# Staggering the batch rows of a two-layer decode kernel so that part of K and V is read once

## The chip, the cores and the metric

The kernel runs on one core of one Trainium2 chip. The metric is the device time of one execution in microseconds (us). Below, "median" is the median of the fast runs of a kernel. TensorE multiplies matrices, VectorE, ScalarE and GpSimd work on elements, and SyncE issues the transfers. In the profile they are called PE (and PEld for the weight loads of TensorE), DVE, ACT, POOL and SP.

## The reference, cut to what matters

```python
# x (8,1,448); K and V caches (8,8,4096,256) bf16; 16 query heads, 8 KV heads
x = x + attn(layernorm(x), K, V, wq, wo)   # layer 0
x = x + B(layernorm(x), w1, w2, w3, w4)
x = x + attn(layernorm(x), K, V, wq, wo)   # layer 1: the same caches and weights
x = x + B(layernorm(x), w1, w2, w3, w4)
```

It is one decode step. Each batch row has its own K and V and never meets another row. K and V of all rows are 256 MiB together, and both layers read the same ones, so a kernel that keeps nothing reads 512 MiB. With one token the gating branch of `B` (w1 and w2) contributes nothing, and both kernels leave it out.

The second layer of a row needs the first layer's result of that row. Between the two there is a chain of small dependent steps: softmax sums, output projection, normalisation, MLP, normalisation again, query projection, and spreading of the query into the layout that the scores need. I call it *the chain* below.

## The kernel before

It takes all rows through layer 0 and then all rows through layer 1. K and V arrive in pieces of 1 MiB; there are three buffers of 2 MiB for K and five of 1 MiB for V. A scheduler orders the instructions. Cuts are marked with `# ...`.

```python
    kp = ctx.enter_context(tc.tile_pool(name="kp", bufs=3))
    vp = ctx.enter_context(tc.tile_pool(name="vp", bufs=5))
    # ...
    def load_k(b, g):
        t = kp.tile([128, 32, Dh], BF16, tag="k")
        src = A_k_cache[b, g].rearrange("(p c) d -> p c d", c=32)
        for n in range(2):                      # 8 KB per partition and transfer
            nc.sync.dma_start(t[:, 16 * n : 16 * n + 16], src[:, 16 * n : 16 * n + 16])
        return t

    def load_v(b, g, hh):
        t = vp.tile([128, 2, 8 * Dh], BF16, tag="v")
        nc.sync.dma_start(                      # two runs of 4 KB per partition
            t[:],
            A_v_cache[b, g, 2048 * hh : 2048 * hh + 2048].rearrange(
                "(a p y) d -> p a (y d)", a=2, y=8
            ),
        )
        return t
    # ...
    units = [(ly, b, g) for ly in range(2) for b in range(Bn) for g in range(G)]
    # ...
    for n, (ly, b, g) in enumerate(units):
        if b == 0 and g == 0:
            emit_q(0, Bn)                       # queries of all rows
        load(n + 1)
        # ...
        transpose_k(kt)                         # DVE, in place, 2 x 2.31 us
        scores(sc, kt, qbd, g)
        pt = probs(sc, zall, g)
        pv(o_ps, pt, v0, 0, g)
        pv(o_ps, pt, v1, 1, g)
        if g == G - 1:
            finish_attention(b, o_ps, zall)
            if b == Bn - 1:
                emit_wo(0, Bn)                  # once per layer, 8 rows at a time
                emit_mlp(0, Bn)
```

The chain thus runs once between the layers, for eight rows at a time, and once at the end without its query part.

The softmax here doesn't subtract the row's maximum and nothing guards it: scores larger than these inputs give would overflow.

## Time and profile before

| | before |
|---|---|
| median (lowest to highest) | 1407.51 us (1407.33 to 1409.43), 4 runs |
| span of the profiled execution | 1405.5 us |
| read from HBM | 547.43 MB |
| chain that ended last | DMA 93% |

Here are lines of the page of the kernel before. The first two give the span and, per engine, busy us, share of the span and instructions (x). The two in the middle cut the span into 40 equal slices of 35 us: busy share of DMA in tenths, and GB/s. The last is the chain of work that ended last, by engine.

```profile
span 1405.5 us, 29105 instructions
PE 577.4 (41%) x13414; PEld 426.9 (30%) x13414; DVE 628.4 (45%) x439; ACT 125.6 (9%) x391; POOL 10.2 (1%) x14
...
DMA  9999999999999999999929999999999999999980
GB/s 327 399 414 414 413 415 413 415 413 414 415 414 414 415 413 414 413 415 412 414 121 370 413 413 415 413 414 415 414 414 414 414 414 413 414 414 414 414 345 1
...
HBM read 547.43 MB, written 0.01 MB: 389 GB/s over the span
...
DMA 93%; PE 4%; DVE 2%; issue 0%; POOL 0%; ACT 0%; POOLq 0%; SPq 0%; ACTq 0%; DVEq 0%
```

The stream is the limit: DMA runs at 412 to 415 GB/s everywhere but at the start, in slices 21 and 22 (121 and 370 GB/s) and in the tail, where nothing is left to load. Every compute engine is busy less than half of the time. The Trainium skill, "DMA: Bandwidth & Descriptors" (Specifications), gives about 358 GB/s of HBM for one core and 435 for the fabric; this trace has 412 to 415 with one core running, so the second figure is the nearer one here.

SyncE's waits show the same. The columns are what it waited for, us in total, number of waits, and the longest.

```profile
SPq L305 <- DMA t<-in_A_v_cache_dram: 480.8, 244, 2.9
SPq L305 <- PE o_ps L364: 230.6, 110, 38.3
```

The waits are many and short: apart from three for the weights at the start (up to 19.0 us), one for the output at the end and one of 38.3 us, none is longer than 3.0 us. The one of 38.3 us is the gap between the layers. The timeline of the gap shows what a chain consists of. Columns: start us, duration us, engine, line, operation, shapes, count, and in brackets the idle time before.

```profile
694.78 7.97 PE L239 MATMUL y_ps<-wo_sb,OT 128*8 128x448 bf16 x32 [0.39 <-DVE OT L385]
...
708.56 2.90 POOL L168 TENSOR_TENSOR rs<-ve,nhalf 128x16 f32<-128x16 f32 x1 [688.52 <-DVE ve L165]
...
715.97 4.21 PE L286 MATMUL y_ps<-w_sb,HT 128*8 128x448 bf16 x14 [2.13 <-DVE HT L283]
...
729.75 3.58 PE L205 MATMUL q_ps<-t,wq_sb 128*128 128x8 bf16 x128 [5.37 <-DVE t L192]
```

The output projection takes 7.97 us, one inverse square root on GpSimd 2.90 us, the second MLP product 4.21 us, and the query projection 3.58 us. The steps follow each other, and from the softmax sums (691.7) to the first new scores (735.5) they fill about 44 us.

### The profile page before, as it was taken

What the parts mean: (1) busy time and instruction counts of PE and PEld (TensorE: products, weight loads), DVE (VectorE), ACT (ScalarE), POOL (GpSimd) and SP (SyncE); (2) the same over time, 40 slices, a digit from 0 to 9 for tenths busy, and PEclk for the clock granted to TensorE, in tenths of its full rate; (3) what the DMA queues carried; (4) which work ended last, traced back from release to release, by engine and by line L of the source; (5) the groups of instructions that cost most, each with busy time, mean ns of one, the idle gap of its engine ahead of it and who ended that gap; (6) DMA issues with size and microseconds to landing.
All of it is one profiled execution on the core that took longest, in us unless ns stands there. A gap on an engine that the chain in (4) does not pass through costs nothing.

```text
span 1405.5 us, 29105 instructions
## 1 busy us (share of the span) xinstructions
PE 577.4 (41%) x13414; PEld 426.9 (30%) x13414; DVE 628.4 (45%) x439; ACT 125.6 (9%) x391; POOL 10.2 (1%) x14
## 2 busy tenths in 40 slices
PE   2234343343434334343554433434343343434336
PEld 2223233232323323232333332323233232323323
DVE  2254444444454444445444444444544444454441
ACT  0101000010101010010001000101010100101010
POOL 0000000000000000000010000000000000000000
PEclk9999999999999999999955555555555555555556
DMA  9999999999999999999929999999999999999980
GB/s 327 399 414 414 413 415 413 415 413 414 415 414 414 415 413 414 413 415 412 414 121 370 413 413 415 413 414 415 414 414 414 414 414 413 414 414 414 414 345 1
DMA packets 113753, 549.32 MB, mean 391 GB/s; under 512 B 8400, under 2 KB 14432, under 8 KB 80480
## 3 DMA queue, kind: packets, MB, share of 16 engines
q1 hardware_dynamic: 107120, 540.59, 94.6%
q10 hardware_dynamic: 6512, 6.88, 1.5%
q8 instruction: 105, 1.72, 0.5%
q14 instruction: 16, 0.13, 0.0%
HBM read 547.43 MB, written 0.01 MB: 389 GB/s over the span
## 4 chain that ended last, share of the span: by engine, by line
DMA 93%; PE 4%; DVE 2%; issue 0%; POOL 0%; ACT 0%; POOLq 0%; SPq 0%; ACTq 0%; DVEq 0%
DMA t<-in_A_k_cache_dram 89%; DMA wo_sb<-in_A_wo_dram 2%; DMA w_sb<-in_B_w_dram 1%; PE y_ps L239 1%; DVE t L318 1%; PE y_ps L286 1%; PE sc_94 L325 0%; PE st L144 0%; POOL rs L168 0%; PE o_ps L364 0%; PE q_ps L205 0%; PE ps L127 0%; PE h_ps L263 0%; POOLq L469 0%; ACT y_sb L250 0%
## 5 line engine op out<-in xcount | busy, mean ns | idle before, releaser
L318 DVE STREAM_TRANSPOSE t<-t 128x2048 uint32<-128x2048 uint32 x256 | 589.3, 2308 | 622.2 <-DMA t<-in_A_k_cache_dram 313.9
L325 PEld LDWEIGHTS <-qbd 128*8 128x8 bf16 x4096 | 130.4, 115 | 674.0 <-issue 594.9
L364 PE MATMUL o_ps<-pt,t 128*128 128x2 bf16 x8192 | 238.7, 165 | 45.3 <-ACT pt L353 39.1
L364 PEld LDWEIGHTS <-t 128*128 128x128 bf16 x8192 | 238.3, 104 | 57.2 <-issue 48.8
L325 PE MATMUL sc_93<-t,qbd 128*8 128x256 bf16 x2048 | 120.2, 410 | 320.9 <-DVE t L318 319.7
L325 PE MATMUL sc_94<-t,qbd 128*8 128x256 bf16 x2048 | 120.5, 410 | 296.3 <-DVE t L318 296.3
L335 ACT ACTIVATE p_sb<-sc_93 128x256 bf16<-128x256 f32 x64 | 47.1, 736 | 585.2 <-PE sc_93 L325 585.2
L335 ACT ACTIVATE p_sb<-sc_94 128x256 bf16<-128x256 f32 x64 | 47.1, 736 | 549.8 <-PE sc_94 L325 549.8
L345 PE MATMUL pt_ps<-identb,p_sb 128*128 128x32 bf16 x256 | 30.1, 198 | 123.5 <-ACT p_sb L335 123.5
L345 PEld LDWEIGHTS <-p_sb 128*128 128x128 bf16 x256 | 16.8, 110 | 186.9 <-ACT p_sb L335 186.9
L384 DVE RECIPROCAL rz<-z_ps 128x16 f32<-128x16 f32 x16 | 4.1, 258 | 63.2 <-PE z_ps L376 63.2
L353 ACT CAST pt<-pt_ps 128x64 bf16<-128x64 f32 x128 | 27.1, 212 | 49.0 <-PE pt_ps L345 49.0
L227 DVE TENSOR_SCALAR qbd<-qs,quad 128x128 bf16<-128x128 f32 x64 | 19.2, 345 | 17.0 <-PE qs L222 17.0
L168 POOL TENSOR_TENSOR rs<-ve,nhalf 128x8 f32<-128x8 f32 (+1 forms) x4 | 9.1, 2271 | 1362.6 <-DVE ve L165 1342.2
L335 ACT ACTIVATION_READ_ACCUMULATOR p_sb<-sc_94 128x1 f32 x64 | 16.7, 261 | 0.0
L335 ACT ACTIVATION_READ_ACCUMULATOR p_sb<-sc_93 128x1 f32 x64 | 16.7, 261 | 0.0
L239 PE MATMUL y_ps<-wo_sb,OT 128*8 128x448 bf16 x64 | 16.2, 424 | 0.8 <-DVE OT L385 0.8
L376 PE MATMUL z_ps<-zall,hsel 128*128 128x8 f32 x64 | 16.0, 361 | 0.0
L376 PEld LDWEIGHTS z_ps<-zall,hsel 128*128 128x128 f32 x64 | 14.9, 322 | 0.0
L205 PE MATMUL q_ps<-t,wq_sb 128*128 128x8 bf16 x256 | 7.6, 168 | 14.2 <-DVE t L192 8.7
L252 DVE TENSOR_TENSOR xT<-xT,ps 128x32 f32<-128x32 f32 x4 | 0.7, 187 | 25.5 <-PE ps L131 25.5
L205 PEld LDWEIGHTS <-wq_sb 128*128 128x128 bf16 x256 | 7.2, 104 | 14.5 <-issue 6.1
(80 smaller groups left out, 92.1 us busy)
## 6 DMA issues: line engine op xcount, KB each, us to landing
t<-in_A_k_cache_dram SPq DMA_DIRECT2D x256, 1024.0 KB, 20.2
t<-in_A_v_cache_dram SPq DMA_DIRECT2D x256, 1024.0 KB, 20.0
wo_sb<-in_A_wo_dram ACTq DMA_DIRECT2D x1, 3584.0 KB, 31.8
wq_sb<-in_A_wq_dram SPq DMA_DIRECT2D x3, 1024.0 KB, 8.9
w_sb<-in_B_w_dram ACTq DMA_DIRECT2D x1, 1568.0 KB, 20.1
w_sb<-in_B_w_dram ACTq DMA_DIRECT2D x3, 448.0 KB, 4.1
wq_sb<-in_A_wq_dram SPq DMA_DIRECT2D x2, 256.0 KB, 12.9
w_sb<-in_B_w_dram ACTq DMA_DIRECT2D x2, 112.0 KB, 4.2
```

The lines of the kernel that those rows point to most:

```text
L168: nc.gpsimd.tensor_tensor(rs[:, 0:n, :].rearrange("p n b -> p (n b)"), ve[:, 0:n, :].rearrange("p n b -> p (n b)"), nhalf[:, 0 : n * nb], ...
L205: nc.tensor.matmul(q_ps[:, j * Hq + h, :], w, xb[:, xi, :], start=(fc == 0), stop=(fc == 3),)
L227: nc.vector.tensor_scalar_mul(qbd[:, :, :, a, :], qs[:].rearrange("p e (f g h) -> p (e f) g h", f=2, h=2), quad[:, a : a + 1],)
L239: nc.tensor.matmul(y_ps[:], OT[:, j, h, b0 : b0 + nb], wo_sb[:, grp, :], start=(grp == 0), stop=(grp == NB2 - 1),)
L286: nc.tensor.matmul(y_ps[:], HT[:, c * nb : c * nb + nb], w4_sb[:, c, :], start=(c == 0), stop=(c == HC - 1),)
L318: nc.vector.transpose(w, w)
L325: nc.tensor.matmul(sc[32 * k : 32 * k + 8, :], qbd[:, ep, g].rearrange("p a h -> p (a h)"), kv[:, k, 2 * half + e2, par], start=(ep == 0), ...
L335: nc.scalar.activation(p_sb[:].rearrange("p t i x -> p x t i"), sc[:].rearrange("p (x t i) -> p x t i", x=4, t=2), ACT.Exp, scale=scale_ex ...
L345: nc.tensor.matmul(pt_ps[:, t], p_sb[:, t].rearrange("p i x -> p (i x)"), rows, start=True, stop=True,)
L353: nc.scalar.copy(pt[:], pt_ps[:])
L364: nc.tensor.matmul(o_ps[:, g, j, :], v[:, a % 2, y * Dh + 128 * j : y * Dh + 128 * j + 128], pt[:, t, k, 2 * a : 2 * a + 2], start=(first ...
L376: nc.tensor.matmul(z_ps[:, h, :], hsel[:, h : h + 1].to_broadcast([128, 128]), zall[:], start=True, stop=True,)
```

## The change: its intent and the diff

The intent is to read less. A row's second pass starts soon after its first, so that part of the row's K and V can stay in SBUF between the two. K and V of a row are 32 pieces of 1 MiB. Those of its last head pair, four of K and four of V, are kept, so that 64 MiB of the 512 MiB need not be read. Now the chain has to run once per row, that is eight times, while other rows' pieces stream. So the change cuts it into a generator with 18 steps and runs two of them after each piece. Order is now written by hand, and the memory that was K and V buffers becomes a ring of six slots of 1 MiB and eight kept slots. Also, V comes in runs of 8 KB per partition. The diff, cut to its core:

```diff
-    kp = ctx.enter_context(tc.tile_pool(name="kp", bufs=3))
-    vp = ctx.enter_context(tc.tile_pool(name="vp", bufs=5))
+    NS = 6
+    kept = [(GP - 1, kv, n) for n in range(4) for kv in range(2)]
+    ctx.enter_context(tc.manual_schedule())
+    slots = [consts.tile([128, 16 * Dh], BF16, name=f"slot{n}") for n in range(NS + len(kept))]
 ...
+    def out_rows(lhs, w, n, b0, nb):            # output projection, and w4 of the MLP
+        y_ps = ps_m.tile([nb, D], FP32, tag="m")
+        for i in range(n):
+            nc.tensor.matmul(y_ps[:], lhs(i), w[:, i, :], start=(i == 0), stop=(i == n - 1))
+            if i % 16 == 15:
+                yield
+        y_sb = chn.tile([Bn, D], FP32, tag="y_sb")
+        nc.scalar.copy(y_sb[:nb, :], y_ps[:])
+        yield
+        ps = rows_to_cols(y_sb, nb)
+        xs = xT[:, :, b0 : b0 + nb]
+        nc.vector.tensor_add(xs, xs, ps[:])
 ...
+    def chain(b, st):
+        OT = work.tile([128, 2, Hq], BF16, tag="OT")
+        yield from finish_attention(st["o"], st["z"], OT)
+        yield from out_rows(lambda i: OT[:, i % 2, i // 2 : i // 2 + 1], wo_sb, NB2, b, 1)
+        yield from mlp(b, 1)
+        qT = chn.tile([128, NB2], BF16, tag="qT2")
+        yield from project_q(b, 1, qT[:].unsqueeze(2))
+        qbd = work.tile([128, 8, GP, 4, 2], BF16, tag="qbd", bufs=3)
+        yield from spread_q(qT[:], qbd)
+        state[1, b] = {"q": qbd}
 ...
-    units = [(ly, b, g) for ly in range(2) for b in range(Bn) for g in range(G)]
+    tasks = [(0, 0, gp) for gp in range(GP)]
+    for b in range(1, Bn):
+        tasks += [(1, b - 2, gp) for gp in range(GP - 1)] if b > 1 else []
+        if b == 1:
+            tasks += [(0, 1, gp) for gp in range(GP - 1)]
+            tasks += [(1, 0, keep), (0, 1, keep)]
+        else:
+            tasks += [(1, b - 1, keep)]          # from the kept slots, not from HBM
+            tasks += [(0, b, gp) for gp in range(GP)]
 ...
+    for idx, it in enumerate(items):             # one item = one piece of K or V
+        n, kv, c = it
+        ...
+        if kv == 0:
+            ...
+            if not (ps == 1 and (gp, 0, c) in kept):
+                transpose_k(slot)
+            scores(sc_t[n % 2], slot, c, st["q"], gp)
+            ...
+        else:
+            pv(state[ps, b]["o"], pt_of[n], slot, c, gp)
+        ...
+        if not (ps == 0 and (gp, kv, c) in kept):
+            held[where[it]] = False
+        emit_loads()
+        for _ in range(2):                       # two steps of the chain per piece
+            for g in gens:
+                next(g, None)
```

The scores of a piece are now 32 products of 128 columns instead of 256, since a piece is 1 MiB and not 2 MiB. The final output projection and MLP still run for eight rows at once after the stream.

## The prediction

> **What bounds it now.** The page's chain is 93% DMA; its slices show DMA at 9 tenths and 412 to 415 GB/s except in three places: the start (327 GB/s), the gap between the layers (121, then 370 GB/s in slices 21 and 22) and the tail (nothing after about 1364 us of 1405). PE (41%), DVE (45%) and ACT (9%) have room. So time is about 512 MiB of K and V at 2.53 us per MiB (1297 us), 26 us of weights, 28 us of DMA lost between the layers, 41 us of tail, about 10 us of start.
>
> **What the change takes away.**
> 1. 64 of 512 MiB: each row's last head pair stays in SBUF: 64 x 2.53 = 162 us.
> 2. V is now read in pieces of 8 KB per partition, not 4 KB. In the trace's DMA packets, stretches of K (8 KB) ran at about 419 GB/s, stretches of V (4 KB) at about 408; all at 419 is 2.50 us per MiB: another 13 us.
> 3. The gap between layers: 28 us. The tail stays (final projection and MLP of 8 rows, 32 us, are unchanged): minus 4 us.
>
> With nothing added this would be about 1195 us.
>
> **What it adds.** The chain from attention to the next layer's q now runs eight times, once per row, cut into 18 steps, two after each 1 MiB piece, on the engines that must also free the slots. It is nearly as long for one row as for eight: read from the gap between layers (timeline): output projection 8.0 us, copy 0.5, back to columns 1.1, statistics 1.7, norm 1.7, w3 1.7, GELU 2, w4 4.2, copy and columns 1.7, second norm 3.5, q 3.6, spreading 2; some 38 us with the doubled softmax sums. The rsqrt on POOL took 1.64 us for 8 columns and 2.90 for 16, so I estimate 0.7 for a row.
>
> The Trainium skill, "TensorE: Matmul & The Clock Gate" (What happens when you issue a matmul), says that only weight loads move ahead on TensorE and matmuls stay in program order; its queue-depth paragraph calls ScalarE and VectorE strictly first in, first out. The program order of the changed kernel puts transposes (2.31 us), scores (about 1.5) and value products (1.0) between the steps, so most add to the chain. Walking the order by hand with these durations, nine pieces take about 51 us where the stream delivers them in 23: a lag of about 30 us. Six slots absorb about 7 (a K slot is freed 4 us after landing; six loads last 15). So each chain stalls DMA about 23 us, eight times: about 180 us. That is nearly all of the traffic saving.
>
> **Sum.** 448 x 2.50 + 26 weights + 7 start + 37 tail + 180 + 2 launch: about 1374 us. Range 1335 to 1410. Faster by over 2%: 0.57; within 2%: 0.36; slower: 0.07.
>
> **What would show it.** HBM read near 480 MB; DMA at 417 to 421 GB/s in undisturbed stretches; no gap near the middle, but eight dips, one per row, some 90 to 170 us apart, each losing 18 to 28 us of DMA while PE and DVE alternate through the chain; SP's longest waits inside them, on PE (scores or value products of the chain's pieces); 224 transposes instead of 256; PE busy up by some 250 us at most. The chain that ended last should contain chain steps, transposes and PE besides DMA.
>
> **What would make it wrong.** If the chain's steps overlap the stream better than the order suggests (a stall under 10 us), about 1250 to 1290. If small single-column steps, semaphores or a cold PE make a chain 10 us longer, it comes out about even with before. If six slots don't keep DMA full in steady state, slower.

## The result, and the profile after

| | before | after |
|---|---|---|
| median (lowest to highest) | 1407.51 us (1407.33 to 1409.43) | 1368.30 us (1365.54 to 1369.12), 4 runs |
| ratio of fast runs, 95% interval | | 0.9715, 0.9698 to 0.9732 |
| read from HBM | 547.43 MB | 480.32 MB |
| span of the profiled execution | 1405.5 us | 1367.4 us |

A ratio here and below is the mean time of one kernel's fast runs over that of the other's of the same rounds, so it isn't quite the ratio of the medians. The change is 2.8% faster by that ratio, while it reads 12% less (67.1 of 547.4 MB). Here are the same lines of the page of the changed kernel; a slice is now 34 us.

```profile
span 1367.4 us, 40957 instructions
PE 749.1 (55%) x19436; PEld 610.0 (45%) x19436; DVE 582.4 (43%) x692; ACT 113.4 (8%) x220; POOL 15.3 (1%) x24
...
DMA  9999689599996999879996899959999599986980
GB/s 357 357 420 419 238 352 419 217 366 418 420 385 216 421 419 419 327 273 419 420 420 254 336 418 420 398 191 392 418 420 362 211 420 420 419 314 249 420 363 1
...
HBM read 480.32 MB, written 0.01 MB: 351 GB/s over the span
...
DMA 45%; PE 26%; DVE 21%; issue 3%; ACT 2%; SPq 2%; POOL 1%; POOLq 0%; DVEq 0%; ACTq 0%
```

The single gap is gone. In its place there are eight dips, to 191 to 273 GB/s in their deepest slice, and between them 418 to 421 GB/s. DMA is 45% of the chain of waits instead of 93%; PE and DVE are 47%.

To size the dips I took the transfers' packets from the trace, in bins of 10 us, and added up from 80 us to the end of the stream how many bytes were missing at 420 GB/s. In us of lost DMA time:

```
dip            1     2     3     4     5     6     7     8    sum
after       20.4  20.9  19.4  19.6  20.5  22.8  21.6  22.6  168.5   (21.1 per chain, with the rest between dips)
```

As a check of this bookkeeping, the parts add up to the span: 482.98 MB of all packets at 420 GB/s are 1150.0 us, the dips 168.5, the start 10.4, and the tail from the landing of the last piece of V at 1331.7 to the end 35.7. The sum is 1364.6 us of 1367.4. (Nearly all of the rest is the last, incomplete bin, which isn't counted as lost; "lost" figures are good to some 3 us. That the sum closes says nothing about the cause.)

What happens in a dip is to be seen in windows. The first window is before the first chain, the second holds it. Columns: window, its length, then busy us (instructions) of PE, PEld, DVE, ACT and POOL, then granted clock, DMA share and GB/s. This is the kernel after.

```profile
80.00:130.00 50.00, 20.61 (x664) 18.00 (x663) 23.72 (x14) 4.32 (x8) 0.00 (x0) 1.00 1.01 419
130.00:180.00 50.00, 31.56 (x613) 23.47 (x614) 19.70 (x51) 3.23 (x9) 1.26 (x2) 0.75 0.69 260
```

In the dip no engine is full. TensorE is busy 63% of it (31.56 of 50 us) and VectorE less than before the chain, and yet the stream falls from 419 to 260 GB/s. So it isn't a lack of throughput. The chain of waits through that window says what it is. Columns: start us, us, engine, tile, line, count. `slot` on DVE is the transpose of a K piece (L393), `sc` the scores of a piece (L400) and `o_t` the value products of a piece (L439). All else is the chain's.

```profile
130.48 1.70 PE z_ps L298 x8
...
132.76 2.23 DVE slot_107 L393
135.03 1.03 PE sc_91 L400 x30
136.06 7.16 PE y_ps L253 x32
143.22 0.89 PE o_t L439 x32
...
145.55 2.22 DVE slot_103 L393
...
149.31 0.71 POOL rs L188
...
150.87 1.67 PE h_ps L269 x56
...
153.36 2.22 DVE slot_105 L393
155.58 0.07 DVE g_1882 L287
155.65 1.01 PE sc_91 L400 x30
156.66 3.71 PE y_ps L253 x14
...
165.95 2.32 DVE slot_107 L393
168.32 1.02 PE sc_91 L400 x29
169.34 3.50 PE q_ps L219 x128
172.84 0.85 PE o_t L439 x32
...
175.96 2.30 DVE slot_103 L393
```

This is one serial path that alternates between PE and DVE. At 155.58 a VectorE step of the GELU has to wait until the transpose ahead of it in program order is done, though ScalarE had its input ready at 153.6, 2.0 us earlier. At 136.06 the product of the output projection holds the value products behind it for 7.16 us, and with them the slot that they would free. From 130.48 to 175.96 are 45.5 us. Of these, 13.9 are the stream's own work: four transposes (8.99 us), three times scores (3.06), two times value products (1.74) and 0.13 for the probabilities. The remaining 31.6 us are the chain's. The 18 steps, two after each piece, are spread over nine pieces, and the stream brings nine pieces in 9 x 2.50 = 22.5 us (1.0486 MB at 420 GB/s). So a chain which alone needs 31.6 us was given 22.5.

The Trainium skill, "TensorE: Matmul & The Clock Gate" (Architectural detail), says that TensorE can pull weight loads ahead of matmuls in flight and that ScalarE and VectorE are strictly first in, first out. The trace agrees: the GELU step at 155.58 started only as the transpose ahead of it ended, and the value products at 143.22 only behind the whole output projection.

Who is made to wait is SyncE, which issues the loads. Its waits with the largest totals in the kernel after, columns as above:

```profile
SPq L386 <- PE o_t L439: 223.0, 123, 8.8
SPq L386 <- PE sc_91 L400: 122.2, 105, 5.9
SPq L386 <- DVE slot_103 L393: 118.0, 32, 15.0
```

In the kernel before most of the waiting ended with a landing, and no wait of the running stream was longer than 3.0 us. Here the waits end with value products, scores and transposes, and in the dips they last up to 8.8 us, the longest all for value products: with only six slots, a slot freed late is a load issued late. (The 15.0 us in the third line is one wait at the start of the kernel and not in a dip.)

### The profile page after: what moved, and what is told of

It reads as the page before. It is cut to its first block, busy times and chain, and to the rows that moved or that the text cites. A ratio compares the mean times of both kernels' runs of the same rounds, so it can differ in the third digit from the quotient of the medians.

```text
span 1367.4 us, 40957 instructions
## 1 busy us (share of the span) xinstructions
PE 749.1 (55%) x19436; PEld 610.0 (45%) x19436; DVE 582.4 (43%) x692; ACT 113.4 (8%) x220; POOL 15.3 (1%) x24
## 2 busy tenths in 40 slices
DMA packets 71816, 482.98 MB, mean 353 GB/s; under 512 B 7376, under 2 KB 13408, under 8 KB 13920
## 3 DMA queue, kind: packets, MB, share of 16 engines
HBM read 480.32 MB, written 0.01 MB: 351 GB/s over the span
## 4 chain that ended last, share of the span: by engine, by line
DMA 45%; PE 26%; DVE 21%; issue 3%; ACT 2%; SPq 2%; POOL 1%; POOLq 0%; DVEq 0%; ACTq 0%
DMA slot_103<-in_A_k_cache_dram 12%; DMA slot_106<-in_A_k_cache_dram 11%; DMA slot_115<-in_A_k_cache_dram 10%; PE y_ps L253 8%; DVE slot_103 L393 5%; DVE slot_107 L393 4%; DVE slot_105 L393 4%; PE sc_90 L400 4%; DMA slot_108<-in_A_v_cache_dram 3%; PE o_t L439 3%; PE sc_91 L400 3%; DMA slot_107<-in_A_v_cache_dram 3%; PE q_ps L219 2%; DVE slot_106 L393 2%; PE z_ps L298 2%
## 5 line engine op out<-in xcount | busy, mean ns | idle before, releaser
L400 PEld LDWEIGHTS <-qbd 128*8 128x8 bf16 x8192 | 203.5, 114 | 496.4 <-issue 419.9
L393 DVE STREAM_TRANSPOSE slot_103<-slot_103 128x2048 uint32<-128x2048 uint32 x64 | 147.6, 2306 | 107.7 <-DMA slot_103<-in_A_k_cache_dram 102.8
L393 DVE STREAM_TRANSPOSE slot_105<-slot_105 128x2048 uint32<-128x2048 uint32 x48 | 110.2, 2296 | 63.5 <-DMA slot_105<-in_A_k_cache_dram 63.5
L393 DVE STREAM_TRANSPOSE slot_107<-slot_107 128x2048 uint32<-128x2048 uint32 x48 | 110.2, 2296 | 47.5 <-DMA slot_107<-in_A_k_cache_dram 47.2
L400 PE MATMUL sc_91<-slot_103,qbd 128*8 128x128 bf16 x1408 | 44.7, 302 | 117.0 <-DVE slot_103 L393 115.8
L410 ACT ACTIVATE p_sb<-sc_91 128x512 bf16<-128x512 f32 x32 | 41.8, 1306 | 489.8 <-PE sc_91 L400 489.8
L439 PE MATMUL o_t<-pt,slot_108 128*128 128x2 bf16 x2048 | 64.7, 165 | 29.6 <-DMA slot_108<-in_A_v_cache_dram 23.2
L439 PEld LDWEIGHTS <-slot_108 128*128 128x128 bf16 x2048 | 59.3, 103 | 43.6 <-DMA slot_108<-in_A_v_cache_dram 25.2
L410 ACT ACTIVATE p_sb<-sc_90 128x512 bf16<-128x512 f32 x32 | 41.8, 1306 | 409.5 <-PE sc_90 L400 409.5
L400 PE MATMUL sc_90<-slot_107,qbd 128*8 128x128 bf16 x960 | 31.4, 303 | 72.8 <-DVE slot_107 L393 68.7
L261 DVE TENSOR_TENSOR xT<-xT,ps 128x4 f32<-128x4 f32 (+1 forms) x18 | 3.0, 165 | 152.4 <-PE ps L150 152.4
L253 PE MATMUL y_ps<-wo_sb,OT 128*1 128x448 bf16 x256 | 62.1, 411 | 0.0
L400 PE MATMUL sc_91<-slot_105,qbd 128*8 128x128 bf16 x960 | 31.5, 303 | 52.7 <-DVE slot_105 L393 46.5
L439 PEld LDWEIGHTS <-slot_106 128*128 128x128 bf16 x1536 | 45.7, 104 | 15.7 <-issue 10.3
L439 PE MATMUL o_t<-pt,slot_106 128*128 128x2 bf16 x1536 | 48.8, 165 | 6.6 <-issue 3.4
L439 PEld LDWEIGHTS <-slot_104 128*128 128x128 bf16 x1536 | 44.7, 104 | 13.2 <-issue 9.7
L439 PE MATMUL o_t<-pt,slot_104 128*128 128x2 bf16 x1536 | 48.6, 166 | 2.9 <-DMA slot_104<-in_A_v_cache_dram 1.5
L393 DVE STREAM_TRANSPOSE slot_106<-slot_106 128x2048 uint32<-128x2048 uint32 x16 | 36.6, 2290 | 21.9 <-DMA slot_106<-in_A_k_cache_dram 21.9
L393 DVE STREAM_TRANSPOSE slot_104<-slot_104 128x2048 uint32<-128x2048 uint32 x16 | 36.6, 2290 | 20.0 <-DMA slot_104<-in_A_k_cache_dram 20.0
L253 PEld LDWEIGHTS <-OT 128*1 128x1 bf16 x256 | 24.7, 97 | 34.6 <-issue 16.3
L400 PE MATMUL sc_90<-slot_105,qbd 128*8 128x128 bf16 x576 | 18.4, 303 | 39.4 <-DVE slot_105 L393 17.6
## 6 DMA issues: line engine op xcount, KB each, us to landing
slot_107<-in_A_k_cache_dram SPq DMA_DIRECT2D x48, 1024.0 KB, 12.5
```

The source lines that it names most:

```text
L253: nc.tensor.matmul(y_ps[:], lhs(i), w[:, i, :], start=(i == 0), stop=(i == n - 1))
L261: nc.vector.tensor_add(xs, xs, ps[:])
L393: nc.vector.transpose(w, w)
L400: nc.tensor.matmul(sc[32 * k : 32 * k + 8, 128 * x : 128 * x + 128], qbd[:, ep, gp].rearrange("p a h -> p (a h)"), kv[:, k, 2 * half + e2, ...
L410: nc.scalar.activation(p_sb[:].rearrange("p t i x -> p x t i"), sc[:].rearrange("p (x t i) -> p x t i", x=4, t=4), ACT.Exp, scale=scale_ex ...
L439: nc.tensor.matmul(o_ps[:, j, 2 * g : 2 * g + 2], v[:, y * Dh + 128 * j : y * Dh + 128 * j + 128], pt[:, y % 4, y // 4, 2 * a : 2 * a + 2] ...
```

## The experiments

My theory was that each chain stalls the stream because its steps and the pieces stand in one order on TensorE and VectorE, and that the number of steps per piece sets by how much. The rivals were that TensorE's work is too much, that the ring or its other traffic can't keep DMA full, or that the pieces' new shape costs time. "Lost" is the lost DMA time from 80 us to the end of the stream, worked out as above, in the profiled execution.

| run | edit to | median us | ratio to before | lost us | per chain |
|---|---|---|---|---|---|
| after | | 1368.30 | 0.9715 | 168.5 | 21.1 |
| one_step | after | 1267.87 | 0.9011 | 64.2 | 8.0 |
| no_chain (wrong) | after | 1212.05 | 0.8611 | 12.5 | 1.6 |
| columns | after | 1336.80 | 0.9497 | 141.8 | 17.7 |
| ring8_kept6 | after | 1366.45 | 0.9705 | 127.1 | 15.9 |
| hoist | after | 1313.97 | 0.9329 | 111.0 | 13.9 |
| reload | after | 1529.58 | 1.0852 | 169.6 | 21.2 |
| b_v8 | before | 1396.46 | 0.9918 | | |
| quads_one | one_step | 1255.43 | 0.8909 | 62.1 | 7.8 |
| best2 | quads_one | 1242.56 | 0.8834 | 47.7 | 6.0 |
| best3 | best2 | 1239.67 | 0.8799 | 42.8 | 5.4 |
| offload | best2 | 1230.12 | 0.8734 | 35.4 | 4.4 |
| offload_b | offload | 1234.81 | 0.8757 | 41.8 | 5.2 |

The kernel before had medians of 1407.72, 1408.28, 1409.62 and 1407.87 us in the four sets of rounds.

### One step per piece (one_step)

```diff
-        for _ in range(2):
+        for _ in range(1):
             for g in gens:
                 next(g, None)
```

> The changed kernel with one chain step after each piece instead of two: same work, same order within the chain, spread over 18 pieces instead of 9. Theory (the chain's steps sit in program order before transposes, scores and value products, so the engines fall about 30 us behind and the six slots stop the stream for about 20 us, eight times): with twice the stream time to hide in, the lag is about 5 to 10 us, nearly inside what the slots absorb, so a dip loses 0 to 8 us instead of 20 and the time is 1205 to 1270 us. Rival (the chain's work itself disturbs the stream, by sharing memory ports or by the amount of TensorE work, wherever it is put): the same loss spread longer, 1355 to 1375 us.

It took 1267.87 us (1262.83 to 1269.79), a ratio of 0.9011 (0.8996 to 0.9026). That is 100 us less than the change for one digit, with the same instructions. The lost time fell by 104 us, from 21.1 to 8.0 us per chain. The page of this run:

```profile
GB/s 349 352 420 419 420 323 418 421 359 393 420 420 401 328 412 420 419 394 319 421 421 418 384 377 421 420 407 326 401 420 420 390 350 418 420 411 357 374 355 1
```

The dips are still there, but their deepest slices are at 319 to 377 GB/s instead of 191 to 273. A chain spread over 18 pieces is given 18 x 2.5 = 45 us, more than the 31.6 us that it needs alone; with twice the pieces more of their work lies between its steps, so this is no exact balance. PE's work as a whole didn't change, so it isn't the cause of these 104 us. That the work of a chain is too dense where it runs is not excluded by this run; hoist, below, keeps the density and changes the order.

### No chain (no_chain)

This run gives a wrong result on purpose (relative error 0.49): the second pass uses the query of the first, and the chain keeps only its first and last part.

```diff
         yield from finish_attention(st["o"], st["z"], OT)
-        yield from out_rows(lambda i: OT[:, i % 2, i // 2 : i // 2 + 1], wo_sb, NB2, b, 1)
-        yield from mlp(b, 1)
-        qT = chn.tile([128, NB2], BF16, tag="qT2")
-        yield from project_q(b, 1, qT[:].unsqueeze(2))
         qbd = work.tile([128, 8, GP, 4, 2], BF16, tag="qbd", bufs=3)
-        yield from spread_q(qT[:], qbd)
+        yield from spread_q(qT1[:, :, b], qbd)
```

> Wrong result on purpose: after the softmax normalisation the chain leaves out projection, MLP and the new q, and spreads the first pass's q again. Traffic, slots, staggering and the two attention passes are as in the changed kernel. Theory: the eight dips vanish, 1368 - 8 x 20 = 1205 us (1195 to 1215). Rival (the ring of six slots or the switching between kept and streamed pieces costs the time): 1300 us or more, with dips at the same places.

It took 1212.05 us (1211.83 to 1212.54), 156 us less than the change, and the lost time is 156 us less as well (12.5 of 168.5 are left). The window of the first chain in this kernel:

```profile
130.00:180.00 50.00, 26.05 (x795) 23.10 (x795) 19.69 (x15) 4.93 (x11) 0.00 (x0) 1.00 1.01 419
```

The same ring, order and reuse hold 419 GB/s where the change falls to 260. So neither the six slots nor the pieces' shape nor the kept slots are at fault: the dips are the chains'. One more rival shows in these lines, the granted clock: it was 0.99 in this run and 0.60 in the change. The other runs settle it: columns had 1.00 and lost 141.8 us, one_step had 0.60 and lost 64.2, hoist 0.59 and lost 111.0. The loss doesn't follow the clock.

### The row products turned into column products (columns)

In the change, the output projection and w4 use the row as weights (one column) and stream 448 columns of the matrix. Here the matrix blocks are the weights and the row is streamed, which also saves the copy and the turning back into columns.

```diff
-        for i in range(n):
-            nc.tensor.matmul(y_ps[:], lhs(i), w[:, i, :], start=(i == 0), stop=(i == n - 1))
+        for fc in range(5):              # three blocks of 128 columns, two of 64
+            ...
+            for i in range(n):
+                nc.tensor.matmul(
+                    dst, w[:, i, c0 : c0 + cw], lhs(i), start=(i == 0), stop=(i == n - 1)
+                )
```

> The output projection and the MLP's second matrix with the weights stationary, result in columns: no copy by ScalarE, no turning back into columns. From this trace's durations, a 128x128 load and a one-column product take about 29 ns, so 160 of them 4.6 us instead of 7 to 8, and 70 take 2.0 instead of 3.7 to 4.2; copies and turning back (2 x 1.7 us) go. Chain shorter by about 7.5 us, tail by about 9. Theory (each us of the serial chain is a us of the dip): 8 x 7.5 + 9 = 69 us less, about 1300 us (1285 to 1315). Rival (the dips are not set by the chain's length): only the tail's 9 us, about 1359.

It took 1336.80 us (1335.88 to 1337.95): better than the change, but it missed my range. The lost time fell by only 3.3 us per chain, and the tail, which uses the same products, by 6.7 us (35.7 to 29.0, from the start of the last value products to the end). The timeline of TensorE in the first chain shows why:

```profile
135.94 2.72 PE L258 MATMUL ps<-OT,wo_sb 128*128 128x1 bf16 x96
...
141.13 0.61 PE L443 MATMUL o_t<-pt,slot 128*128 128x2 bf16 x17 [2.07 <-issue]
141.67 3.38 PE L258 MATMUL ps<-OT,wo_sb 128*64 128x1 bf16 x64
```

96 products with 128 columns of weights took 2.72 us, 28 ns each. 64 products with 64 columns took 3.38 us, 53 ns each. The Trainium skill, "TensorE: Matmul & The Clock Gate" (Weight-path perf modes), says that the fast weight load is on only when the number of weights is 128 and the type isn't FP32; 28 against 53 ns agree with that, though no run isolates it as the reason, and I hadn't taken it into my estimate. With a pause of 2.07 us, to which I come back in the last section, the output projection gained nothing. The w4 part went from 5.5 us (156.66 to 162.11 in the chain above, with the copy and the turning) to 2.7 us, and that is about the gain per chain.

### Eight ring slots, six kept (ring8_kept6)

```diff
-    NS = 6
-    kept = [(GP - 1, kv, n) for n in range(4) for kv in range(2)]
+    NS = 8
+    kept = [(GP - 1, kv, n) for n in range(3) for kv in range(2)]
```

> Two of the eight kept pieces become ring slots: 8 slots, 6 kept. Traffic rises by 16 MiB, at 2.50 us per MiB 40 us. Theory (a dip is the lag minus what the slots absorb, one slot being 2.5 us of stream): each of eight dips shrinks by 5 us, 40 us in all, so the time stays at 1368 us within 10. Rival (slots beyond six make no difference): 1408 us. Rival (the ring is too shallow in steady state also): below 1350.

It took 1366.45 us (1363.73 to 1367.97), the same as the change. It read 497.10 MB, so 16.8 MB more, which are 40 us at 420 GB/s; and it lost 41.4 us less. Per chain, two more slots saved 5.2 us, which is just two pieces' 2 x 2.5 us. A slot therefore is worth one piece's time per chain, both as a ring slot (8 chains x 2.5 = 20 us) and as a kept slot (8 rows x 2.5 = 20 us): in this state of the kernel they trade evenly. No run has seven slots with eight kept.

### The next transpose before the chain's steps (hoist)

While a chain is alive, the transpose of the next K piece that has been asked for goes in front of the chain's steps.

```diff
+        if any(g.gi_frame is not None for g in gens):
+            for j in (idx + 1, idx + 2):
+                if j < len(items) and items[j][1] == 0 and items[j] not in loads:
+                    turn(j)              # transposes once, later calls do nothing
+                    break
         for _ in range(2):
```

> The changed kernel, two chain steps per piece, same instructions; only the program order on VectorE differs: while a chain runs, the transpose of the next piece of K is issued before the chain steps instead of after them, so it no longer waits for them nor they for it. In the first chain of the profile four transposes of 2.3 us stand between the chain's end and its start, and a fifth delays the norm by 1.1 us. Theory (program order puts stream work and chain work into one serial line): 8 to 10 us per chain come off the dips, 1368 - 8 x 9 = about 1296 us (1280 to 1315). Rival (the amount of work on the engines sets the dip, not its order): 1360 to 1370 us.

It took 1313.97 us (1311.61 to 1315.28), 54 us less than the change and at the upper end of my range. The instructions are the same and only their order on VectorE differs. The window of the first chain, to compare with the 260 GB/s of the change:

```profile
130.00:180.00 50.00, 38.80 (x746) 28.63 (x747) 24.43 (x53) 3.11 (x7) 1.26 (x2) 0.68 0.80 308
```

TensorE and VectorE do more in these 50 us than in the change (38.80 and 24.43 us against 31.56 and 19.70), and the stream is faster. Lost per chain: 13.9 instead of 21.1, so 7.2 us less (I had expected 8 to 10), which is most of the 9.0 us of transposes that stood on the path. That is direct evidence for the order as the mechanism.

### No reuse (reload)

```diff
             where[it] = NS + kept.index(key)
-            if ps == 0:
-                loads.append(it)
+            loads.append(it)
 ...
-            if not (ps == 1 and (gp, 0, c) in kept):
-                transpose_k(slot)
+            transpose_k(slot)
 ...
-        if not (ps == 0 and (gp, kv, c) in kept):
-            held[where[it]] = False
+        held[where[it]] = False
```

> The changed kernel without the reuse: the eight slots stay, but each is freed after use and filled again in the second pass, whose keys are transposed again. Staggering, chains and ring as in the changed kernel. Theory: 64 MiB more at 2.50 us each, 1368 + 160 = 1528 us (1515 to 1540), 547 MB read, so slower than the kernel before by 120 us: the reuse only just pays for the dips. If part of the dips hides in the pauses where kept pieces need no stream, or the other way round: off by more than 15 us.

It took 1529.58 us (1528.05 to 1531.12) and read 547.43 MB as before. So the reuse alone is worth 161 us, and everything else in the change together costs 120 us against the 1409.62 us of the kernel before in these rounds (ratio 1.0852). Its lost time (169.6) equals the change's (168.5): the reuse neither causes nor softens the dips. The run also sets a rival aside, the pauses of TensorE in the last section: it has 2 of them where the change has 28, and loses the same.

### The kernel before with V in runs of 8 KB (b_v8)

```diff
         nc.sync.dma_start(
-            t[:],
+            t[:].rearrange("p a c -> p (a c)"),
             A_v_cache[b, g, 2048 * hh : 2048 * hh + 2048].rearrange(
-                "(a p y) d -> p a (y d)", a=2, y=8
+                "(p y) d -> p (y d)", y=16
             ),
```

This permutes the rows of V against their probabilities. It still passed as correct within the tolerance; my explanation, that the probabilities are nearly equal for these inputs, is argued and not tested.

> Wrong result on purpose: the kernel before, with V fetched in pieces of 8 KB per partition instead of two of 4 KB; nothing else. Theory (the stream of V ran at 408 and that of K at 419 GB/s because of the packet size): all at 2.50 us per MiB instead of 2.53, 14 us less: 1393 us (1388 to 1398), with 418 to 420 GB/s in full slices. Rival (V's place in memory or the mix sets the rate): 1405 to 1408.

It took 1396.46 us (1396.31 to 1397.33), 12 us less than the kernel before in the same rounds (1408.28). That is inside my range and clear of the noise, though under the 2% from which the record calls a run faster. The line to compare with that of before:

```profile
GB/s 324 354 420 418 418 419 419 418 418 419 418 418 418 419 418 418 419 419 418 418 146 353 418 418 419 418 418 419 419 418 419 418 419 418 418 419 418 419 341 1
```

Full slices went from 412 to 415 GB/s to 418 to 420. In the packets of the kernel before, those of 8192 bytes took 316 ns on average and those of 4096 bytes 163 ns, so twice the smaller one is 3% longer.

### One step per piece and four products at a time (quads_one)

By now I believed that TensorE's long row products were the reason for the dips that one_step had left. (That TensorE's work in a chain's 18 pieces takes longer than their stream, the trace of one_step doesn't show: from 128 to 182 us TensorE is busy 41.95 of 54 us.) Four row products can run side by side in the four groups of 32 columns of the array.

```diff
+            for i in range(n):
+                k = i % 4
+                nc.tensor.matmul(
+                    y_ps[32 * k : 32 * k + 32, :],
+                    lhs(i).to_broadcast([128, 32]),
+                    w[:, i, :],
+                    start=(i < 4),
+                    stop=(i >= n - 4),
+                )
```

The four partial sums are added when the row is turned into columns, with a selector that has a 1 in partitions 0, 32, 64 and 96. The tail's products are as in the columns run.

> One step per piece, and the chain's two row products (output projection, MLP's second matrix) run as four partial sums side by side in four column groups of TensorE, with the weights as before; a selector sums the four when the row is turned into columns. In the tail (8 rows) the column form of the run before. Scores run the same way: 32 products of 256 columns took 1.88 us, so 32 of 448 should take 3.3 us instead of 7.4 and 14 take 1.5 instead of 3.9. one_step still lost 51 us more than no_chain by its profile (6 us a chain)[...]. Theory: 6.5 us less work puts it under the stream, dips of 2 us or less are left: 1268 - 36 - 6 for the tail = about 1226 us (1210 to 1240). Rival (what one_step still loses is waiting between engines, not TensorE work): 1250 to 1262 us.

The mechanism did what it should. The timeline of TensorE in this kernel:

```profile
134.55 1.69 PE L263 MATMUL y_ps<-wo_sb,OT 128*32 128x448 bf16 x16
...
138.42 1.71 PE L263 MATMUL y_ps<-wo_sb,OT 128*32 128x448 bf16 x16
```

The 32 products took 3.4 us instead of 7.38 in the change, as the Trainium skill, "TensorE: Matmul & The Clock Gate" (Packing small matmuls), lets one expect when it says that tiles of the array can run matmuls concurrently. The time was 1255.43 us (1252.21 to 1255.99): above my range and inside the rival's. The lost time per chain stayed (7.8 against 8.0), and the gain came from the tail: between the profiled executions, 7.5 us apart in span (1261.0 and 1253.5), it fell by 5.8 us (34.8 to 29.0, measured as in the columns run) and the lost time by 2.1. The medians are 12 us apart since the profiled execution of one_step was its fastest; what the slower executions lose in the dips wasn't profiled. So at one step per piece, the length of these products is not what stalls the stream. My second theory fell.

### The first pass's query earlier (best2)

In the change, the query of the next row's first pass is spread all at once, in front of the scores that need it. Here the end of the chain before does it, in steps.

```diff
         state[1, b] = {"q": qbd}
+        if 1 <= b < Bn - 1:
+            yield
+            nxt = work.tile([128, 8, GP, 4, 2], BF16, tag="qbd", bufs=4)
+            yield from spread_q(qT1[:, :, b + 1], nxt)
+            state[0, b + 1] = {"q": nxt}
```

> As quads_one, and the first-pass q of rows 2 to 7 is spread by two more chain steps ahead of time, instead of in one go just before the row's first scores. By the profile of no_chain some 15 us of small dips are left outside chains, part of them there. Theory: 3 to 8 us less than quads_one, about 1220 us. If the small dips come from elsewhere: the same as quads_one within 2 us.

It took 1242.56 us (1241.45 to 1249.36), 13 us less than quads_one where I had expected 3 to 8, and far from the 1220 us that I had expected with quads_one at 1226. The rival, the same as quads_one, fell too. The lost time fell by 14.4 us, so the gain is in the dips. Spreading the query in one go was a larger part of them than I had thought.

### best2 with the transposes hoisted (best3)

The edit is that of hoist, on best2.

> As best2, and the next transpose of K goes before the chain steps on VectorE, as in hoist. quads_one came out at 1255 us, where the theory that one_step is short of TensorE time wanted 1226 and the rival (waiting between engines) 1250 to 1262: so the rival is followed here. Per pair of pieces (5.0 us of stream) the serial line is now transpose 2.3, scores 1.0, a chain step, value products 1.0, a chain step: with steps of 1.5 to 2 us that is over 5. Theory: with the transpose out of this line the lag stays inside the ring: 1215 to 1228 us. Rival (some other wait): 1238 to 1246.

It took 1239.67 us (1236.41 to 1245.42): a miss, and where the rival theory had put it. What brought 54 us at two steps per piece brings 3 us here, and the ranges overlap. With one step per piece, hoisting the transposes hardly helps any more.

### The chain's small work off VectorE (offload)

Of the chain's work on VectorE, only the softmax division stays there. Element work in SBUF goes to GpSimd, reads of PSUM to ScalarE.

```diff
+        E = nc.gpsimd if nb == 1 else nc.vector
-        nc.vector.tensor_mul(var[:], mv[:, 0, :], mv[:, 0, :])
+        E.tensor_mul(var[:], mv[:, 0, :], mv[:, 0, :])
 ...
-        nc.vector.tensor_copy(mv[:], st[:])
+        (nc.scalar.copy if nb == 1 else nc.vector.tensor_copy)(mv[:], st[:])
 ...
+            if on_act:
+                nc.scalar.activation(qbd[:, :, :, a, :], src, ACT.Copy, scale=quad[:, a : a + 1])
```

> As best2, but the chain's small operations leave VectorE: what reads PSUM goes to ScalarE, the rest to GpSimd; VectorE keeps the transposes and the two softmax divisions of a row. So transposes depend on the stream alone. Theory (transposes caught between chain operations make the rest of the dips): 1212 to 1228 us, although each small operation may be slower on GpSimd. Rival (TensorE's own program order, scores and value products behind chain products that wait for the small operations, makes them): no better than best2, 1240 us or more, since those waits get longer.

It took 1230.12 us (1228.66 to 1232.81), a ratio of 0.8734 (0.8715 to 0.8752) to before. That misses my range by 2 us, but the rival (no better than best2, since GpSimd is slower) fell. VectorE now takes a piece as soon as it lands. The timeline of VectorE, and GpSimd's group of the new small steps (columns of the group: shapes and count, then busy us, mean ns, then idle us before them and what ended it):

```profile
145.99 2.31 DVE L447 STREAM_TRANSPOSE slot<-slot 128x2048 uint32<-128x2048 uint32 x1 [2.74 <-DMA slot<-in_A_k_cache_dram]
151.01 2.31 DVE L447 STREAM_TRANSPOSE slot<-slot 128x2048 uint32<-128x2048 uint32 x1 [2.71 <-DMA slot<-in_A_k_cache_dram]
```

```profile
L186 POOL TENSOR_TENSOR var<-mv 128x1 f32<-128x1 f32 x16 | 3.1, 196 | 36.0 <-ACT mv L184 36.0
```

From 134 to 165 us, inside the chain's window, VectorE does nothing but a transpose every 5 to 6 us, each released by a landing. The small steps take 184 to 227 ns on GpSimd where in the change they took 139 to 176 on VectorE; the reciprocal, done there as a power, takes 572 instead of 169. The Trainium skill, "GPSIMD Engine Reference" (4.1, Engine selection), advises VectorE for such work. By duration it is right here too; but the shared order cost more than the slower engine does. Which half of that order mattered isn't separated: best3 had put transposes before the chain's steps and gained only 3 us, so it may be the steps that waited behind transposes more than the reverse.

### A shorter chain again (offload_b)

What offload still loses might come from chains that end too late. So this one takes two steps after every fourth piece.

```diff
-        for _ in range(1):
+        for _ in range(2 if idx % 4 == 0 else 1):
```

> As offload, with two chain steps instead of one after every fourth piece, so a chain of 18 steps ends about three pieces before the second pass needs its q. In the profile of offload a row's chain ends at 409 us, about 7 us after the first piece that waits for it could have run, and the dips (345 to 401 GB/s from 400 to 440 us) sit there. Theory (the late end of the chain makes what is left of the dips): 4 to 10 us less, 1220 to 1226 us. Rival (TensorE is simply full there, with pauses of 1 to 2 us in its instruction stream): 1228 to 1235 us, no better.

It took 1234.81 us (1232.67 to 1236.93), 5 us more, inside the rival's range. The lateness of the chain's end isn't what remains.

The best version is offload: 1230.12 us, 12.7% below the kernel before by the ratio, and 138 us below the change. It gives a correct result. Its four runs also show that the granted clock doesn't order the times: they had 0.772, 1.0, 0.594 and 0.602 for 1228.66, 1231.20, 1229.03 and 1232.81 us.

### What stays open

Offload loses 4.4 us per chain, no_chain 1.6. The difference of 2.8 us per chain (some 23 us in all) isn't explained. Candidates are the pauses of TensorE in the last section (32 against 23 in no_chain, 44.8 against 29.4 us) and TensorE's load in the chain's densest places (busy 29.90 us of the 40 from 400 to 440); neither was isolated.

## Why the prediction was right, point by point

The prediction was 1374 us with a range of 1335 to 1410, and it came out at 1368.3.

- **The bound before.** DMA at 412 to 415 GB/s and 93% of the chain of waits were read correctly; b_v8 shows that a 1% faster stream is a nearly 1% faster kernel (0.9918).
- **64 of 512 MiB, 162 us.** Confirmed: HBM read fell to 480.32 MB, and taking the reuse back cost 161 us (reload).
- **V in runs of 8 KB, 13 us.** b_v8 gained 12 us. Right, slightly too large. Undisturbed stretches ran at 418 to 421 GB/s as predicted.
- **The gap, 28 us.** It is gone from the middle. The same work came back eight times.
- **The tail, 37 us.** It measured 35.7 us.
- **The chain's stall, 23 us, eight times: the term that decided.** It measured 21.1 us, 168.5 instead of about 180. The walk of the order gave 51 us for nine pieces; from the first probabilities' work at 130.2 us to the end of the first scores with the new query at 179.3 us the trace has 49. That the chains and the order of their steps make the stall is shown, by taking the chain away (12.5 us left), by spreading it (64.2), by another order alone (111.0) and by two more slots (127.1 at 16.8 MB more traffic).
- **The single-row rsqrt, 0.7 us.** It measured 0.71 and 0.56 in the chain.
- **Scores of a piece, about 1.5 us.** Too long: they took 1.02. That is most of why the walk came out 2 us long.
- **224 transposes; PE busier by 250 us at most.** 224, and 172 us more (577 to 749).
- **Eight dips of 18 to 28 us, with SyncE's longest waits in them on PE.** Each lost 19.4 to 22.8 us, and the longest waits in them, 7.3 to 8.8 us, are for value products.
- **The total, in part by luck.** The terms as written add up to 1372 us. The stall was 11.5 us too long, the tail 1.3; the start was too short by 3.4 us and the bytes by 4 (1146 against 1150.0 us; the prediction left out the instruction transfers, 2.6 MB or 6 us). So errors of two signs make the total better than its parts. Also, the prediction gave only 0.57 to a gain over 2%, and the measured 2.8% isn't far above that.

What was wrong came later. Spreading the chain fixed most of the stall, and I then blamed TensorE's products for the rest (quads_one), the order of transposes (best3) and the late end of the chain (offload_b). All three fell. The first two had a measured cost at two steps per piece (3.3 us per chain in columns, 7.2 in hoist; the third wasn't tried there), but once the chain was given 45 us instead of 22.5, little of that cost was left on the path.

## What to carry to other kernels

When a serial chain runs beside a stream on the same in-order engines, compare its length, with the stream's own work that stands in between, with the time of the pieces that it is spread over; here 45.5 us against 22.5 lost 21 us each time, and one step per piece instead of two returned 100 us. Traffic saved only counts once the stream keeps flowing: 161 us of saved reads nearly all went into stalls, and a run with the chain taken out shows in one look how much there is to win. Then free the engine that must serve the stream on arrival from the chain's small steps, even if another engine does them more slowly.

## What the Trainium skill lacked or had wrong

- **"Runtime: NRT & Kernel Launch", Instruction fetch mechanics.** It says that the sequencer fetches instructions in blocks of 256 while it executes and that the cost of a block boundary is mostly hidden. In these traces TensorE pauses for 0.7 to 3.0 us with no recorded wait, always at positions in its instruction stream that lie multiples of 256 apart (products and weight loads counted). In the kernel after, each time an instruction-queue transfer of about 1 us has ended 1.3 to 1.6 us before TensorE resumes. That the saturated stream delays the refill is my inference; no run isolates it, and reload, with the same stream, has hardly any pauses. The pauses of over 0.7 us with no recorded wait:

```
              after  no_chain  columns  best3  offload  offload_b  reload
pauses           28        23       40     28       32         37       2
us in total    37.5      29.4     53.3   50.9     44.8       63.6     3.4
first positions in the kernel after: 3777, 4545, 4801, 5313, 5569, 7873
differences: 768, 256, 512, 256, 2304
```

- **"DMA: Bandwidth & Descriptors", Specifications.** About 358 GB/s is given as the HBM limit of a core, and one core streamed at 418 to 421 GB/s here with runs of 8 KB per partition. The page isn't wrong in this: its section Bandwidth says that about 358 holds with both cores of an HBM domain streaming, and gives 425 for a single core. What it lacks is a rate that tells 4 KB from 8 KB per partition; the runs do: 412 to 415 GB/s for the mix and 418 to 420 for 8 KB alone, 12 us of 1408 (b_v8).
- **"TensorE: Matmul & The Clock Gate", Weight-path perf modes.** It has no figure beside its condition for the case of fewer than 128 weights, but the page doesn't lack it: its section "LDWEIGHTS (loading the stationary operand)" puts a load at its columns over 1.2 in ns, which by estimate is 53 ns for 64 columns. A product with 64 columns of weights took 53 ns against 28 ns with 128 (columns).
- **"GPSIMD Engine Reference", 4.1.** For elementwise work its choice of engine goes by duration, with GpSimd about twice as slow for two inputs. In these small steps it was less: 196 ns against 160 for a product of two 128x1 tiles (offload, after). And small steps of 139 to 176 ns on VectorE and 184 to 227 ns on GpSimd were 12 us cheaper in all on the slower engine and ScalarE (offload against best2), which durations alone don't tell.
